# Score products of 512 columns issued as two matmuls of 256 with the same weights

## The chip, the cores and the metric

The kernel runs on one core of a Trainium2 chip, as one launch. A time is the device time of one execution in microseconds (us), and the median of several executions stands for a kernel. The core has five engines that run beside each other and wait for one another through semaphores: PE (TensorE, matmuls; its weight loads have a row of their own in the profile, PEld), DVE (VectorE), ACT (ScalarE), POOL (GpSimd) and SP (SyncE, which here issues most of the DMAs).

## The reference, cut to what matters

Four layers follow each other on a sequence of 2048 rows of 512 values, each with a residual: x = x + A(layernorm(x)), then B, then A, then B. A is a Fourier mixing: products with the DFT matrices of the hidden and of the sequence dimension, of which the real part is kept. B is attention with a compressed memory, in 32 heads of 16 values and 4 segments of 512 rows:

```python
for s in range(N):                                  # 4 segments, L = 512 rows each
    qs, ks, vs = q[:, :, s], k[:, :, s], v[:, :, s]
    logits = jnp.einsum("bhqd,bhkd->bhqk", qs, ks) * scale + mask   # causal mask
    p = _softmax(logits, axis=-1)
    a_dot = jnp.einsum("bhqk,bhkd->bhqd", p, vs)
    pq = phi(qs)                                    # phi(t) = t + 1 if t > 0 else exp(t)
    a_mem = (pq @ M) / (pq @ z + 1e-6)
    outs.append(g * a_mem + (1.0 - g) * a_dot)
    M, z = M + phi(ks).T @ vs, z + sum(phi(ks))
```

The change touches the logits, the products of queries and keys.

## The kernel before, in words

Everything is float32 to the outside. Most matmuls are made of three fp32r products of split values, high and low part (`matmul3`, line 107). The Fourier layers (lines 190 to 452) and the projections of attention are such products with 512 moving columns.

Attention (`place_attention`, line 454) works in units of four heads of one segment: 4 segments times 8 units, 32 units in each of the two attention layers, 64 in all. Queries and keys are split into three bf16 parts, written to DRAM and read back as stacks, `stkq` and `stkk` (`stack`, line 561), in which the parts stand one over another in 96 rows, so that one bf16 matmul with 96 rows gives a score with nearly float32 precision. A unit reads its stack twice:

- `natural_max` (line 581) computes scores with a row of queries on each partition, for query tiles i = 0 to 3 of 128 rows each. The weights are the query tile, the moving operand is the keys up to it: 128, 256, 384 or 512 columns. Two short products share a PSUM bank of 512 columns: 128 with 384, and 256 with 256 of two heads (the tile `nat`). DVE then adds the mask and takes the maximum of each row (line 603).
- `max_rows` (line 632) transposes these maxima and writes them, split in three bf16 rows, under the queries of the stack, where they are rows 97 to 99 (`KROWS` is 96, `K` 99).
- `softmax_values` (line 647) computes the scores again, with keys on the partitions and the maximum already taken off (tile `sT`). Weights are the key tile kt, moving columns are the queries from it on: 512, 384, 256 or 128. Again 384 shares a bank with 128, and 256 with 256 of the next head. ACT clips the diagonal blocks (Relu, line 668) and takes the exponent (line 669), POOL zeroes what the mask hides (line 672), and PE multiplies with the values (`pv`, line 682).

So each unit has four products of 512 columns in either form (i = 3, and kt = 0), 8 in all, and 512 in the kernel.

The order of the work is written out by slots: `place` (line 177) puts a step of a generator into a numbered slot, and at the end (lines 1056 to 1059) the slots run in order, within a slot by a rank. PE's instructions keep this program order (`in_order`, line 83). The other engines' order is the scheduler's, which goes by program order and by priorities: `tc.high_priority(offset=URGENT)` moves an instruction forward by a number of instructions (URGENT is 150, line 41). Besides the lines above, the prediction speaks of `prep` (line 458), which loads rows of the layer's input as `xt`, normalises them to `xn` (line 159) and transposes them for the next segment; of the output product (`po`, line 860, with the split values `oh`); and of SP's queue, which issues the loads of `xt`, the stacks and the parts in one order. In the prediction "fp32r" names the products of split values, "bf16" the scores.

Of the kernel before, what the change touches and what calls it, by code (L numbers as in the profile page):

```python
# [18 lines left out]
P = 128  # L19
# [16 lines left out]
KROWS = NSLOT * DH  # L36
# [25 lines left out]
def spectral_infini_kernel(  # L62
# [13 lines left out]
    V, A, G, T = nc.vector, nc.scalar, nc.gpsimd, nc.tensor  # L76
# [6 lines left out]
    def in_order(engine, name):  # L83
        op = getattr(engine, name)

        def call(*args, **kwargs):
            return tc.keep_in_program_order(op(*args, **kwargs))  # L87

        return call

    T = SimpleNamespace(matmul=in_order(T, "matmul"), transpose=in_order(T, "transpose"))
# [15 lines left out]
    def matmul3(ps, lhsT, rhs, first, last):  # L107
        T.matmul(ps, lhsT(0), rhs(0), start=first, stop=False)
        T.matmul(ps, lhsT(0), rhs(1), start=False, stop=False)
        T.matmul(ps, lhsT(1), rhs(0), start=False, stop=last)  # L110

    def rows(ap, i):
        return ap[i * P : (i + 1) * P, :]

    def bank(name, shape=(P, 512), dtype=F32):
        return psum.tile(list(shape), dtype, name=name, tag="bank", bufs=8)

    def pair(name, tag, bufs, dtype=F32R):
        return sb.tile([P, 2, 512], dtype, name=name, tag=tag, bufs=bufs)
# [334 lines left out]
    def place_attention(x_in, x_out, t0, w_at, out_at):  # L454
# [126 lines left out]
        def natural_max(s, g, u):  # L581
            qs, ks = stacks[s, g, u, "q"], stacks[s, g, u, "k"]
            mx = sb.tile([P, HU, LT], F32, name="mx", bufs=2)

            def scores(*cols):
                ps = bank("nat")
                views, off = [], 0
                for h, i in cols:
                    n = (i + 1) * P
                    T.matmul(  # L590
                        ps[:, off : off + n],
                        qs[:KROWS, h, i * P : (i + 1) * P],
                        ks[:KROWS, h, :n],
                        start=True,
                        stop=True,
                    )
                    views.append((ps[:, off : off + n], mx[:, h, i : i + 1]))
                    off += n
                for src, dst in views:
                    n = src.shape[1]  # L600
                    junk = sb.tile([P, 512], BF16, name="junk", bufs=1)
                    with tc.high_priority(offset=URGENT):
                        V.tensor_tensor_reduce(  # L603
                            junk[:, :n], src, mask[:, 512 - n :], 1.0, 3e38,
                            ALU.add, ALU.min, dst,
                        )

            for h in range(HU):
                scores((h, 3))
                yield  # L610
                scores((h, 0), (h, 2))
                yield
                if h % 2:
                    scores((h - 1, 1), (h, 1))
                    yield
            parts = max_parts[((s * NG + g) * (HG // HU) + u) % 2]
            rem = sb.tile([P, HU, LT], F32, name="mrem", bufs=2)
            with tc.high_priority(offset=2 * URGENT):
                V.scalar_tensor_tensor(
                    parts[:, 0], mx, -2.0, mx, op0=ALU.mult, op1=ALU.add  # L620
                )
                for dst in rem, parts[:, 1]:
                    V.scalar_tensor_tensor(
                        dst, mx, -1.0, parts[:, 0], op0=ALU.mult, op1=ALU.subtract
                    )
                V.scalar_tensor_tensor(
                    parts[:, 2], rem, 1.0, parts[:, 1], op0=ALU.mult, op1=ALU.subtract
                )
            maxima[s, g, u] = parts
            yield  # L630
# [16 lines left out]
        def softmax_values(s, g, u):  # L647
            qs, ks = stacks.pop((s, g, u, "q")), stacks.pop((s, g, u, "k"))
            K = KROWS + MROWS
            h0 = g * HG + u * HU  # L650

            def scores(dst, *cols):
                ps = bank("sT")
                off, diag = 0, []
                for h, kt in cols:
                    n = 512 - kt * P
                    T.matmul(
                        ps[:, off : off + n],
                        ks[:K, h, kt * P : (kt + 1) * P],
                        qs[:K, h, kt * P :],  # L660
                        start=True,
                        stop=True,
                    )
                    diag.append(off // P)
                    off += n
                blocks = ps.rearrange("p (b c) -> p b c", c=P)
                blocks = blocks[:, diag[0] : diag[-1] + 1 : max(1, diag[-1] - diag[0])]
                A.activation(blocks, blocks, AF.Relu)  # L668
                A.activation(dst, ps, AF.Exp, scale=-SCALE)  # L669

            def causal(blocks):
                G.affine_select(  # L672
                    blocks,
                    blocks,
                    pattern=[[0, n] for n in blocks.shape[1:-1]] + [[1, P]],
                    compare_op=ALU.is_ge,
                    fill=0.0,
                    base=0,
                    channel_multiplier=-1,
                )  # L680

            def pv(pv_bank, kt, pt, off):
                n = 512 - kt * P
                for h in range(HU):
                    T.matmul(
                        pv_bank[32 * h : 32 * h + VW, kt * P :],
                        vt[s][kt][:, h0 + h, :],
                        pt[h // 2][:, h % 2, off : off + n],
                        start=kt == 0,
                        stop=kt == 2,  # L690
                        skip_group_check=True,
                    )

            p0, p1 = [], []
            events = {}

            def ev(t, f):
                events.setdefault(t, []).append(f)

            for h in range(HU):  # L700

                def first(h=h):
                    if h % 2 == 0:
                        p0.append(pair("pT", "wd", 8, F32))
                    scores(p0[h // 2][:, h % 2], (h, 0))
                    if h % 2:
                        causal(p0[h // 2][:, :, :P])

                ev(6 + h, first)
            for h in range(HU):  # L710

                def second(h=h):
                    if h % 2 == 0:
                        p1.append(pair("pT", "wd", 8, F32))
                    scores(p1[h // 2][:, h % 2], (h, 1), (h, 3))
                    if h % 2:
                        for c in 0, 3 * P:
                            causal(p1[h // 2][:, :, c : c + P])

                ev(2 + h, second)  # L720
            p2 = []
            for h in range(0, HU, 2):

                def third(h=h):
                    if h == 0:
                        p2.append(sb.tile([P, HU, 256], F32, name="pT2", tag="craw", bufs=2))
                    scores(p2[0][:, h : h + 2].rearrange("p h s -> p (h s)"), (h, 2), (h + 1, 2))
                    if h == 2:
                        causal(p2[0][:, :, :P])

                ev(h // 2, third)

            def last():
                pb = pv_banks[0]
                pv(pb, 0, p0, 0)
                pv(pb, 1, p1, 0)
                pv(pb, 3, p1, 384)
                pv(pb, 2, (p2[0][:, :2], p2[0][:, 2:]), 0)
                ot = sb.tile([P, 512], F32, name="ot", tag="ut", bufs=8)
                A.activation(ot, pb, AF.Copy)  # L740
                outs[s, g, u] = ot

            ev(12, last)
            for t in range(13):
                for f in events.get(t, ()):
                    f()
                yield
# [196 lines left out]
        for k in range(4 * DT):  # L944
            n, d = "qkvo"[k // DT], k % DT
# [156 lines left out]
```

## Time and profile before

| | |
|---|---|
| median of 3 timed runs | 1908.67 us (1908.55 to 1909.09) |
| span of the profiled execution | 1911.1 us |
| mean granted clock of TensorE in it | 0.985 |
| instructions, PE / PEld / DVE / ACT / POOL | 10336 / 10336 / 4073 / 2292 / 831 |
| busy, PE / PEld / DVE / ACT / POOL | 95% / 68% / 69% / 56% / 27% |
| DMA | 296.49 MB, mean 155 GB/s |

The profile is of one execution, from its first to its last instruction; it is the only time that stands for this execution, and it is 2.4 us over the median of the timed runs. A row of a group names line, engine, operation, output and inputs, the shapes and the count, then the busy time in us, the mean duration of one in ns, and the idle time of the engine just before these instructions with what ended it. A row of a timeline gives start and duration in us. A matmul has its line in a helper (L87), so tiles tell the groups apart. Ends of matmuls are modelled and successive ones overlap, so a sum of durations is not a time on the engine.

### The profile page before, as it was taken

Reading aid. Unit: us, or ns where it says so; the run is one execution under the profiler, and the core shown is the slowest. Engines: PE = TensorE matmul, PEld = TensorE weight load, DVE = VectorE, ACT = ScalarE, POOL = GpSimd, SP = SyncE. Lnnn points to the kernel's source line nnn. Section 1 sums busy time; section 2 is a strip of 40 time slices with the busy share of each in tenths; the row PEclk is TensorE's granted clock in tenths of the full one; section 3 lists DMA queues with packets and bytes.
Section 4 is the critical chain, followed back from the end, with each engine's and each line's share of the span. In section 5 each row is a group of like instructions: output and inputs, shape, how many; then the busy total and the mean of one; then the engine's idle time right before and its main releaser. Section 6 shows DMA issues by size and latency. Waiting matters only on the chain. (4 is left out here: it accounts for less than half of the span.)

```text
span 1911.1 us, 31877 instructions
## 1 busy us (share of the span) xinstructions
PE 1809.7 (95%) x10336; PEld 1301.0 (68%) x10336; DVE 1311.1 (69%) x4073; ACT 1062.9 (56%) x2292; POOL 512.5 (27%) x831
## 2 busy tenths in 40 slices
PE   7899999999899999999889999999988999999998
PEld 6678888888556656665458888787865655666654
DVE  8654545462787787777866687777558778777773
ACT  3221213331578777767664465453337877777775
POOL 4200000002345344446431000000124443434432
PEclk9999999999899999999999999999999999999998
DMA  6665555353544333434445787563444434444231
GB/s 224 233 208 199 189 191 198 115 173 121 178 125 148 118 120 115 149 119 134 134 154 181 222 251 225 164 204 127 159 150 139 144 108 134 126 133 142 91 117 45
DMA packets 165655, 296.49 MB, mean 155 GB/s; under 512 B 17776, under 2 KB 66928, under 8 KB 165488
## 3 DMA queue, kind: packets, MB, share of 16 engines
q1 hardware_dynamic: 162224, 293.68, 47.5%
q8 instruction: 81, 1.33, 0.3%
q10 hardware_dynamic: 3264, 0.79, 0.2%
q14 instruction: 86, 0.70, 0.1%
HBM read 192.95 MB, written 100.66 MB: 154 GB/s over the span
## 5 line engine op out<-in xcount | busy, mean ns | idle before, releaser
L603 DVE CUSTOM_DVE_ANT_0 junk<-nat,mask 128x512 bf16<-128x512 f32 (+3 forms) x1024 | 496.6, 485 | 203.2 <-PE nat L87 183.9
L669 ACT ACTIVATE pT<-sT 128x512 f32<-128x512 f32 x640 | 370.3, 598 | 15.0 <-ACT sT L668 2.2
L87 PE MATMUL u<-chi,xa 128*128 128x512 f32 x1024 | 321.1, 395 | 10.9 <-DVE xa L97 7.3
L672 POOL TENSOR_SCALAR_AFFINE_SELECT pT<-pT 128x256 f32<-128x256 f32 (+1 forms) x448 | 197.4, 455 | 431.5 <-ACT pT L669 366.8
L87 PE MATMUL sT<-stkq,stkk 99*128 99x256 bf16 (+3 forms) x1024 | 250.7, 307 | 17.5 <-DVE mx L603 8.8
L87 PE MATMUL nat<-stkk,stkq 96*128 96x512 bf16 (+3 forms) x1024 | 246.5, 302 | 20.8 <-DVE mx L603 12.4
L668 ACT ACTIVATE sT<-sT 128x256 f32<-128x256 f32 (+1 forms) x640 | 208.6, 334 | 63.9 <-PE sT L87 56.7
L87 PEld LDWEIGHTS u<-chi,xa 128*128 128x128 f32 x1024 | 195.4, 191 | 52.8 <-issue 7.2
L87 PE MATMUL u<-clo,xa 128*128 128x512 f32 x512 | 202.6, 396 | 9.6 <-DVE clo L101 9.6
L142 POOL TENSOR_TENSOR r<-ve,half_neg 128x2 f32<-128x2 f32 (+1 forms) x33 | 24.0, 728 | 696.5 <-DVE ve L140 692.9
L87 PE MATMUL y<-wdt,us 128*128 128x512 f32 x768 | 182.5, 391 | 1.2 <-DVE wdt L101 1.2
L87 PEld LDWEIGHTS <-stkk 99*128 99x128 bf16 x1024 | 82.6, 99 | 146.3 <-issue 127.9
L87 PEld LDWEIGHTS y<-wdt,us 128*128 128x128 f32 x768 | 143.4, 188 | 31.6 <-DVE wdt L101 2.0
L87 PE MATMUL pv_bank<-pT,vt 128*17 128x128 f32 (+3 forms) x2048 | 158.7, 440 | 1.7 <-POOL pT L672 1.6
L87 PEld LDWEIGHTS <-stkq 96*128 96x128 bf16 x1024 | 94.9, 99 | 75.9 <-issue 37.3
L87 PE MATMUL po<-wo,oh 128*128 128x512 f32 x384 | 125.7, 443 | 7.6 <-DVE oh L101 5.4
L87 PE MATMUL pvv<-wv,xT 128*128 128x512 f32 x384 | 127.0, 443 | 3.9 <-DVE mx L603 3.9
L87 PE MATMUL pqk<-xT,wq 128*128 128x512 f32 x384 | 129.9, 447 | 0.0
L87 PE MATMUL pqk<-xT,wk 128*128 128x512 f32 x384 | 127.8, 442 | 0.0
L87 PEld LDWEIGHTS u<-clo,xa 128*128 128x128 f32 x512 | 97.7, 191 | 32.5 <-DVE clo L101 12.2
L87 PEld LDWEIGHTS pv_bank<-pT,vt 128*17 128x17 f32 x2048 | 57.6, 98 | 90.7 <-issue 77.0
L99 ACT ACTIVATE clo<-cring 128x512 fp32r<-128x512 f32 x112 | 70.6, 631 | 69.1 <-DVE chi L101 37.9
(138 smaller groups left out, 3032.0 us busy)
## 6 DMA issues: line engine op xcount, KB each, us to landing
sum<-sring SPq DMA_DIRECT2D x32, 1024.0 KB
cring<-sum SPq DMA_DIRECT2D x128, 256.0 KB
stkq<-scrq SPq DMA_DIRECT2D x64, 384.0 KB
stkk<-scrk SPq DMA_DIRECT2D x64, 384.0 KB
cring<-in_ct SPq DMA_DIRECT2D x96, 256.0 KB
sring<-in_ct SPq DMA_DIRECT2D x32, 512.0 KB
xt<-mid SPq DMA_DIRECT2D x64, 256.0 KB
craw<-in_ct SPq DMA_DIRECT2D x30, 512.0 KB
```

The costliest lines, as they stand in the source:

```text
L87: return tc.keep_in_program_order(op(*args, **kwargs))
L99: A.activation(hi, src, AF.Copy, scale=scale)
L142: G.tensor_tensor(out=r, in0=ve, in1=half_neg[:, :n], op=ALU.pow)
L603: V.tensor_tensor_reduce(junk[:, :n], src, mask[:, 512 - n :], 1.0, 3e38, ALU.add, ALU.min, dst,)
L668: A.activation(blocks, blocks, AF.Relu)
L669: A.activation(dst, ps, AF.Exp, scale=-SCALE)
L672: G.affine_select(blocks, blocks, pattern=[[0, n] for n in blocks.shape[1:-1]] + [[1, P]], compare_op=ALU.is_ge, fill=0.0, base=0, channel ...
```

## The change

A product of 512 moving columns is issued as two of 256, with the same weights, into the two halves of the same PSUM bank. Products of 128, 256 and 384 columns stay as they are, and so does everything that reads the results.

```diff
+    def halves(n):
+        return ((0, n // 2), (n // 2, n // 2)) if n == 512 else ((0, n),)
...
                     n = (i + 1) * P
-                    T.matmul(
-                        ps[:, off : off + n],
-                        qs[:KROWS, h, i * P : (i + 1) * P],
-                        ks[:KROWS, h, :n],
-                        start=True,
-                        stop=True,
-                    )
+                    for c, w in halves(n):
+                        T.matmul(
+                            ps[:, off + c : off + c + w],
+                            qs[:KROWS, h, i * P : (i + 1) * P],
+                            ks[:KROWS, h, c : c + w],
+                            start=True,
+                            stop=True,
+                        )
...
                     n = 512 - kt * P
-                    T.matmul(
-                        ps[:, off : off + n],
-                        ks[:K, h, kt * P : (kt + 1) * P],
-                        qs[:K, h, kt * P :],
-                        start=True,
-                        stop=True,
-                    )
+                    for c, w in halves(n):
+                        T.matmul(
+                            ps[:, off + c : off + c + w],
+                            ks[:K, h, kt * P : (kt + 1) * P],
+                            qs[:K, h, kt * P + c : kt * P + c + w],
+                            start=True,
+                            stop=True,
+                        )
```

In the built program each bf16 matmul has a weight load instruction of its own, so either half loads the weights again.

## The prediction, made before the changed kernel ran

> **What bounds the kernel now.** I read the first two parts of the page, then the busy time by stretch, then the groups by shape, then the timeline of the score products. The page:
>
> ```profile
> span 1911.1 us, 31877 instructions
> PE 1809.7 (95%) x10336; PEld 1301.0 (68%) x10336; DVE 1311.1 (69%) x4073; ACT 1062.9 (56%) x2292; POOL 512.5 (27%) x831
> ```
>
> PE is the busiest engine by far, and it has one weight load (PEld) for each matmul. The score products stand in the two attention stages; their busy time by stretch (columns: stretch, its us, busy us of PE, PEld, DVE, ACT and POOL with instruction counts, granted clock, DMA share, GB/s):
>
> ```profile
> 500.00:1005.00 505.00, 466.76 (x3230) 293.24 (x3230) 387.64 (x1552) 377.49 (x885) 230.81 (x388) 0.97 0.42 132
> 1415.00:1911.00 496.00, 458.82 (x3233) 287.08 (x3231) 365.85 (x1509) 364.88 (x863) 203.24 (x364) 0.98 0.38 121
> ```
>
> Of these 1001 us PE is idle for 38.2 + 37.2 = 75.4 us. So PE is the bound in both, nine tenths of the time: what lengthens PE's stream there lengthens the kernel, nearly one for one. The groups of the score products, by shape (busy us, mean ns of one):
>
> ```profile
> L87 PE MATMUL sT<-stkq,stkk 99*128 99x512 bf16 x256 | 100.3, 393 | 2.4 <-ACT pT L669 1.4 <-DVE mx L603 1.0
> L87 PE MATMUL nat<-stkk,stkq 96*128 96x512 bf16 x256 | 98.1, 383 | 10.0 <-DVE mx L603 6.2 <-DMA stkk<-scrk 2.7 <-DVE onat L806 0.4
> L87 PE MATMUL sT<-stkq,stkk 99*128 99x256 bf16 x256 | 51.7, 284 | 12.0 <-DVE mx L603 4.9 <-ACT oh L99 2.6 <-DMA stkq<-mt 2.5
> L87 PE MATMUL nat<-stkk,stkq 96*128 96x256 bf16 x256 | 49.6, 275 | 0.0
> ```
>
> These means are not what a product costs the stream. 284 + 284 against 393 looks like a loss of 175 ns for each split, but matmuls are pipelined, and a mean of one contains its way through the array, which lies under the next one. The cost is the time from one start to the next. Happily the kernel already issues pairs of 256 columns, each with its own weight load, beside singles of 512, in the same places of the stream, so that the trace of before holds the very thing that the change makes.
>
> **The change, part by part.** It removes 256 + 256 = 512 matmuls of 512 columns and adds 1024 of 256, with 512 more weight loads. The price of one split comes from start to start. Timeline of PE (start, us, instruction, count); for each kind the first and the last row of those that I averaged, with the row that follows each:
>
> ```profile
> 497.66 0.38 PE L87 MATMUL sT<-stkq,stkk 99*128 99x256 bf16 x2
> 497.88 0.38 PE L87 MATMUL nat<-stkk,stkq 96*128 96x512 bf16 x1
> ...
> 500.19 0.39 PE L87 MATMUL nat<-stkk,stkq 96*128 96x256 bf16 x2
> 500.41 0.38 PE L87 MATMUL sT<-stkq,stkk 99*128 99x384 bf16 x2
> ...
> 524.38 0.39 PE L87 MATMUL sT<-stkq,stkk 99*128 99x512 bf16 x1
> 524.61 0.38 PE L87 MATMUL nat<-stkk,stkq 96*128 96x128 bf16 x2
> ...
> 540.67 0.38 PE L87 MATMUL nat<-stkk,stkq 96*128 96x512 bf16 x1
> 540.89 0.38 PE L87 MATMUL sT<-stkq,stkk 99*128 99x512 bf16 x1
> ...
> 1865.63 0.39 PE L87 MATMUL sT<-stkq,stkk 99*128 99x512 bf16 x1
> 1865.86 0.38 PE L87 MATMUL nat<-stkk,stkq 96*128 96x256 bf16 x2
> 1866.08 0.38 PE L87 MATMUL sT<-stkq,stkk 99*128 99x512 bf16 x1
> ...
> 1868.39 0.39 PE L87 MATMUL sT<-stkq,stkk 99*128 99x256 bf16 x2
> 1868.62 0.38 PE L87 MATMUL nat<-stkk,stkq 96*128 96x512 bf16 x1
> 1868.84 0.38 PE L87 MATMUL sT<-stkq,stkk 99*128 99x256 bf16 x2
> ```
>
> Transposed scores (sT) behind a 512-column fp32r product, at the full clock and without a wait: a single takes 524.61 - 524.38 = 0.23 us at the first and 0.23 at the last, over 154 of them a mean of 227.7 ns (median 227); a pair 0.22 and 0.23, over 69 a mean of 229.5 (median 230). Natural scores (nat) ahead of another bf16 product or a small one: a single 0.22 and 0.22, over 24 a mean of 220.0 (median 219); a pair 0.22 and 0.22, over 59 a mean of 221.5 (median 222). So a split costs 1.5 to 1.8 ns by the means and 3 by the medians. I take 2 ns: 512 x 2 = **+1.0 us**. The bounds are 0 (the last rows of both kinds are alike to the 0.01 us that the timeline shows) and 3 ns, which is 0 and +1.5 us; 2 ns is nearest to the means, and a sum is made of means.
>
> The weight loads lie beside the matmuls:
>
> ```profile
> L87 PEld LDWEIGHTS <-stkq 96*128 96x128 bf16 x1024 | 94.9, 99 | 75.9 <-issue 37.3 <-DVE onat L806 0.7
> L87 PEld LDWEIGHTS <-stkk 99*128 99x128 bf16 x1024 | 82.6, 99 | 146.3 <-issue 127.9 <-DMA stkq<-mt 9.4 <-DVE mx L603 0.9
> ```
>
> A load takes 99 ns, and a half of 256 columns holds the array for some 110 (half of the 0.22 above): the load of the second half fits under the first half. I cost the 512 loads at nothing; the matmul before each hides it, and if that cover were gone they would cost 512 x 99 ns = 50.7 us. [...]
>
> The change adds no wait: in the built program the first half takes over the wait of the single, the second waits for nothing, and only the second half signals. So ACT's Relu of the diagonal block, which reads only columns of the first half in the kt = 0 products, cannot start on the first half; I count no gain there. Readers of a whole product see it 113 + 275 against 383 ns after its start (113 is half of a 0.22 to 0.23 pair, rounded up), so about 5 ns later; if each of the 512 stood on the path, 2.6 us, but DVE and ACT have slack in most places, and I take 0.
>
> What moves on the other engines: PE's order stays as it is but for the halves. About a dozen instructions of DVE, four of ACT, three of POOL and four transfers on SP's queue change places with neighbours, because the scheduler counts the new instructions. The place that matters is where attention prepares its last segment (line 159, xn), in both layers; the first layer's (an [idle before <-releaser] behind a row is that engine's wait):
>
> ```profile
> 676.47 0.32 SPq L574 DMA_DIRECT2D stkq<-scrq  x1
> ...
> 677.50 0.68 DVE L603 CUSTOM_DVE_ANT_0 junk<-nat,mask 128x512 bf16<-128x512 f32 x1
> ...
> 678.11 1.28 DVE L159 TENSOR_SCALAR xn<-xt,mv,rr 128x512 f32<-128x512 f32 x2
> ...
> 678.24 0.38 PE L87 MATMUL sT<-stkq,stkk 99*128 99x256 bf16 x2 [0.67 <-DVE mx L603]
> ...
> 680.25 0.38 PE L87 MATMUL nat<-stkk,stkq 96*128 96x512 bf16 x1 [1.64 <-DVE mx L603]
> ...
> 681.99 1.65 PE L87 MATMUL po<-wo,oh 128*128 128x512 f32 x3 [1.36 <-DVE oh L101]
> ```
>
> One xn (0.64 us) now runs ahead of the 512-column maximum, so PE's wait of 0.67 us grows by 0.64. The next wait, for a maximum behind both xn, ends where it did, and 1.64 shrinks to 1.0: net 0. On SP one load of xt, which waits for that first xn (by these rows it would end near 677.50 + 0.64 = 678.1), goes ahead of the stack loads that left at 676.47, so those leave some 2 us later. The first score product that reads them, and the same two events of a usual unit behind it:
>
> ```profile
> 690.16 0.38 PE L87 MATMUL nat<-stkk,stkq 96*128 96x512 bf16 x1
> ...
> 1652.62 0.33 SPq L574 DMA_DIRECT2D stkq<-scrq  x1
> ...
> 1660.08 0.38 PE L87 MATMUL nat<-stkk,stkq 96*128 96x512 bf16 x1
> ```
>
> 13.7 us of lead become about 11.7, still more than the 7.5 us of the usual unit, where PE does not wait. I take 0 for all moves; their bounds are rivals A and D below.
>
> The sum: 1.0 us on the span of 1911.1 us gives 1912.1. The timed runs have a median of 1908.67, 2.4 us under the profiled span, and I carry the difference over: 1908.67 + 1.0 = **1909.7 us**, +0.05%. About 0.2% (3.8 us) is what a measurement of this kernel can tell from no change.
>
> **The rivals.** *A, slower: a stall that costs the clock.* Right behind the stall above, and behind its like in the second layer, PE runs at half the clock; busy time by stretch:
>
> ```profile
> 678.00:681.10 3.10, 0.75 (x3) 0.19 (x2) 3.06 (x9) 2.87 (x7) 2.44 (x3) 1.00 0.79 177
> 681.10:687.90 6.80, 5.92 (x22) 3.45 (x26) 4.29 (x12) 1.80 (x4) 1.22 (x2) 0.50 0.77 273
> ...
> 1609.50:1612.90 3.40, 3.40 (x17) 2.40 (x19) 2.07 (x6) 0.37 (x2) 0.00 (x0) 0.50 1.06 384
> ```
>
> 6.8 and 3.4 us at 0.50 cost up to 3.4 and 1.7 us. If a moved instruction of DVE makes a stall longer by one xn (0.64) where nothing gives it back, and as much half clock again follows, that is 4.0 us in the first layer and 2.3 in the second: 1908.67 + 1.0 + 6.4 = 1916.1. It decides once PE's idle time in such a place, 3.7 us now (0.67 + 1.64 + 1.36), grows instead of shifting. For it: the moves stand just there. Against: the releasers of the last two waits keep their places.
>
> *B, slower: instructions do not reach PE fast enough.* The densest long stretch and a usual one:
>
> ```profile
> 807.28:827.28 20.00, 20.00 (x165) 13.33 (x164) 15.26 (x63) 13.09 (x31) 7.16 (x14) 1.00 0.49 161
> 1700.00:1800.00 100.00, 98.58 (x723) 64.10 (x722) 75.61 (x317) 77.54 (x183) 46.42 (x83) 1.00 0.42 136
> ```
>
> 329 matmuls and loads in 20 us are one per 60.8 ns; the usual is 1445 in 100 us, 69.2 ns. If 60.8 were a ceiling, the 512 x 2 new instructions would cost up to 62 us where all is that dense; on the average of 69.2 there is room (7% more gives 64.5), so perhaps a fifth of it, 12 us: 1921. Nothing shows PE starved in that stretch (20.00 busy of 20.00), which speaks against. [...]
>
> [...]
>
> *D, faster: the same shuffle goes the other way.* An earlier xn shortens one of PE's waits enough that the half-clock stretch does not come, in both layers: 1908.67 + 1.0 - 3.4 - 1.7 = 1904.6, just past 0.2%. For it: waits there hang on DVE. Against: 1.36 us behind oh remain in any case.
>
> **How the numbers follow.** Forecast (0 to 3 ns for each split, the moves give nothing that lasts) 0.70; A 0.14; B 0.04; C 0.03; D 0.09. Range 1905 to 1917: the upper end takes in A with both layers (1916.1), the lower end all of D's way but its last step; B, C and D, 0.16 in all, are left out. Faster by over 0.2%: D, 0.09; slower: A, B and C, 0.21; within: 0.70.
>
> **What would show it.** In the profile after, PE and PEld should count 10848 each, no score product of 512 columns should be left, and 768 of 256 should stand in either group, the pairs taking 0.22 to 0.23 us from start to next start and the busy time of DVE, ACT and POOL as before. [...] I am wrong about the term itself if the pair of one product, which loads the same weights twice, differs from the pair of two products that I measured.

## The result, and the profile after

| | before | after |
|---|---|---|
| median of 20 runs each, taken in turn on the same chip | 1907.62 us | 1912.21 us |
| lowest and highest run | 1902.87, 1910.96 | 1906.47, 1917.94 |
| span of the profiled execution | 1911.1 us | 1908.5 us |

The ratio is 1.0025, with a 95% interval of 1.0016 to 1.0034: slower by 4.6 us by the medians. The forecast was +1.0 us. The time lies in the range that was given, but just over the 0.2% that the forecast called no change, and the interval reaches down to 0.16%, so the side of that line is not sure. That the change costs something is.

The two profiled executions say the opposite of the medians: after is 2.6 us shorter. The execution profiled for after took 1910.26 us, below the median of its 20 runs, and the one of before lay above its own median. Runs of one kernel spread over 8 to 11 us here, so one profile against one profile decides nothing of this size. What profiles can decide is what the work costs where it stands. The page of after, its busy time by engine:

```profile
span 1908.5 us, 33070 instructions
PE 1806.2 (95%) x10848; PEld 1330.2 (70%) x10848; DVE 1309.1 (69%) x4073; ACT 1062.8 (56%) x2292; POOL 511.8 (27%) x831
```

512 matmuls and 512 loads more; DVE, ACT and POOL have the same instructions and the same busy time to 2 us. The groups of 256 columns (busy us, mean ns of one, idle time before them):

```profile
L87 PE MATMUL sT<-stkq,stkk 99*128 99x256 bf16 x768 | 151.4, 280 | 16.3 <-DMA stkq<-mt 7.5 <-DVE mx L607 6.9 <-ACT pT L674 1.3
L87 PE MATMUL nat<-stkk,stkq 96*128 96x256 bf16 x768 | 148.2, 274 | 7.5 <-DVE mx L607 4.5 <-DMA stkk<-scrk 1.8 <-DVE onat L811 0.4
```

768 in either form, as forecast, and no group of 512 columns is left. The two attention stages (columns as in the prediction):

```profile
500.00:1005.00 505.00, 465.14 (x3496) 307.70 (x3495) 389.51 (x1558) 379.82 (x889) 230.34 (x388) 0.99 0.42 133
1415.00:1908.50 493.50, 458.50 (x3474) 303.18 (x3473) 364.39 (x1506) 363.77 (x862) 202.88 (x363) 0.97 0.39 121
```

PEld is busier by 14 and 16 us, PE by nothing (465.14 us against 466.76, 458.50 against 458.82): the loads lie under the matmuls. PE's timeline in the second attention layer, with the former singles as pairs:

```profile
1687.98 0.38 PE L87 MATMUL nat<-stkk,stkq 96*128 96x256 bf16 x2
1688.12 0.94 PE L87 MATMUL pqk<-xT,wq 128*128 128x512 f32 x3
1688.90 0.40 PE L87 MATMUL sT<-stkq,stkk 99*128 99x256 bf16 x2
1689.13 0.38 PE L87 MATMUL nat<-stkk,stkq 96*128 96x128 bf16 x2
```

The pair of one product takes 1689.13 - 1688.90 = 0.23 us to the next start, as the pairs of two products did in before. A natural pair with the three fp32r products behind it takes 0.92 us.

### The profile page after: what moved, and what is told of

It is laid out like the page before. It is cut to its first block, busy times and chain, and to the rows that moved or that the text cites. A ratio compares the mean times of both kernels' runs of the same rounds, so it can differ in the third digit from the quotient of the medians.

```text
span 1908.5 us, 33070 instructions
## 1 busy us (share of the span) xinstructions
PE 1806.2 (95%) x10848; PEld 1330.2 (70%) x10848; DVE 1309.1 (69%) x4073; ACT 1062.8 (56%) x2292; POOL 511.8 (27%) x831
## 5 line engine op out<-in xcount | busy, mean ns | idle before, releaser
L87 PE MATMUL sT<-stkq,stkk 99*128 99x256 bf16 (+2 forms) x1280 | 250.5, 278 | 17.4 <-DVE mx L607 7.8
L87 PE MATMUL nat<-stkk,stkq 96*128 96x256 bf16 (+2 forms) x1280 | 247.0, 274 | 17.2 <-DVE mx L607 12.1
L87 PEld LDWEIGHTS <-stkk 99*128 99x128 bf16 x1280 | 93.5, 99 | 149.0 <-issue 130.5
L87 PEld LDWEIGHTS <-stkq 96*128 96x128 bf16 x1280 | 113.6, 99 | 60.9 <-issue 33.0
L87 PE MATMUL pvv<-wv,xT 128*128 128x512 f32 x384 | 120.7, 426 | 3.8 <-DVE mx L607 3.8
L87 PE MATMUL pqk<-xT,wk 128*128 128x512 f32 x384 | 122.6, 428 | 0.0
L87 PE MATMUL pqk<-xT,wq 128*128 128x512 f32 x384 | 121.8, 426 | 0.0
L99 ACT ACTIVATE clo<-cring 128x512 fp32r<-128x512 f32 x112 | 70.6, 631 | 69.1 <-DVE chi L101 37.1
```

The costliest lines, as they stand in the source:

```text
L99: A.activation(hi, src, AF.Copy, scale=scale)
```

## The experiments

Theories. **T1**: the split itself costs PE's stream 1 to 5 us. **T2**: the split costs about nothing, and the changed order on the other engines carries the loss, through stalls and the half clock behind them (rival A's mechanism, in some place). Beside them rival B (instructions arrive too slowly) and C (the second load shows) were carried on.

In each comparison the kernel before ran on the same chip in the same rounds; a1 to a4 ran on one chip, b1 to b4 on a second, c1 to c4 on a third. The edit that most kernels share pins an engine's order. The numbers are an engine's instructions in program order, and each gets a scheduling edge, without a semaphore, to its neighbour:

```diff
+    pinned = {
+        "SP": [[210, 211, 247, 214, 213, 212], ...],
+        "DVE": [[847, 1042, 853, 1043, ...], [1281, 1282, 1283, 1410, 1411, 1284], [2436, 2631, ...]],
+        "Activation": [[2293, 2294, 2295, 2297, ...]],
+    }
+    for engine, runs in pinned.items():
...
+            for a, b in zip(run, run[1:]):
+                tc.add_manual_dep(traced[b], traced[a].name, ...)
```

The order of before and that of after differ in four groups of moves: *prep* (DVE's first and third list, and SP's four, both attention layers), *spectral* (DVE's second list: one `xn` of the second Fourier layer's `normalise` ahead of one maximum, and with it two splits on POOL), and the *tail* (ACT's list, near the end). In the traces DVE, ACT, POOL and SP follow the order that each experiment names, instruction for instruction.

### Two by two: the split and the order

**a1**, the kernel before with no edit, shows what the comparison gives for nothing.

> The kernel before, unchanged, as a fourth corner of a table of two by two (products whole or split; the other engines' order of before or of after). Every theory: a ratio of 1.000 to the kernel before, within 0.1%; what it differs by is the noise of the other three.

**a2**, whole products in the order of after:

```diff
+        "DVE": [[847, 1042, 1043, 853, ...], [1281, 1282, 1410, 1283, 1411, 1284], [2436, 2631, 2632, ...]],
```

> Products whole as before, but DVE, ACT, POOL and SP in the order that the scheduler gives them in the changed kernel (pinned). Theory M, that the moved instructions cost what the split does not (the measured 4.6 us less 1.0): a ratio of 1.0019, about +3.6 us. Rival S, that the split itself costs all of the 4.6 us, in ways that one profile does not show: 1.000.

**a3**, the split in the order of before (the first diff above, on the kernel after).

> Products split as in the changed kernel, but DVE, ACT, POOL and SP in the order of the kernel before (pinned). Theory M: only the stream cost of the split, 512 x 2 ns = 1.0 us, a ratio of 1.0005. Rival S: 1.0024, about +4.6 us, 9 ns for each split.

**a4**, the kernel after again, no edit.

> The changed kernel once more. Both theories: 1.0024 as measured; a ratio under 1.001 would mean that the first comparison was of two draws of noise (theory N).

**c4**, a3 once more, on another chip.

> The split with the old order once more, to narrow the cost of the split alone: theory M 1.0005 (+1.0 us), within 1.000 and 1.001; a ratio of 1.0015 or more would put the loss back on the split.

Measured, ratio to the kernel before with its interval:

| | order of before | order of after |
|---|---|---|
| whole | a1 0.9998 (0.9984 to 1.0012) | a2 1.0015 (0.9999 to 1.0030) |
| split | a3 1.0001 (0.9985 to 1.0017), c4 0.9998 (0.9986 to 1.0010) | a4 1.0032 (1.0017 to 1.0046), the result 1.0025 (1.0016 to 1.0034) |

The split alone costs nothing that can be measured, twice; with the new order the loss is there, twice. T1 in its larger sizes falls (the upper ends of a3 and c4 are 3.2 and 1.9 us, which leaves room for the forecast's 1.0), and the order is where the loss lies. The new order on whole products gives 1.0015, which is consistent with anything from nothing to the whole loss.

The split's own cost is best read in a dense stretch. The second attention layer has one from a transposition of maxima (`mT`) to another nine units on, at the full clock, with 72 split products; start of its first and last row in before, in after, and in b4 (below, the same products in quarters):

```profile
1691.61 0.22 PE L87 MATMUL mT<-ident_b,mparts 128*80 128x128 bf16 x1
...
1826.21 0.22 PE L87 MATMUL mT<-ident_b,mparts 128*80 128x128 bf16 x1 [0.17 <-DVE mx L603]
```

```profile
1689.35 0.22 PE L87 MATMUL mT<-ident_b,mparts 128*80 128x128 bf16 x1
...
1823.82 0.22 PE L87 MATMUL mT<-ident_b,mparts 128*80 128x128 bf16 x1 [0.17 <-DVE mx L607]
```

```profile
1689.94 0.22 PE L87 MATMUL mT<-ident_b,mparts 128*80 128x128 bf16 x1
...
1825.46 0.22 PE L87 MATMUL mT<-ident_b,mparts 128*80 128x128 bf16 x1 [0.17 <-DVE mx L607]
```

134.60 us before, 134.47 after, 135.52 in quarters. Nine units of halves cost nothing that this shows; 2 ns each would be 0.14 us, which is about the size by which the two differ in the other direction.

### Which of the moves

**b1**, the split with only the prep moves as in after (the lists for prep are dropped, so the scheduler places these as in after; the others stay pinned):

```diff
-        "SP": [...],
-        "DVE": [[847, ...], [1281, 1282, 1283, 1410, 1411, 1284], [2436, ...]],
+        "DVE": [[1281, 1282, 1283, 1410, 1411, 1284]],
```

> Products split; DVE and SP in the new order where attention prepares its last segment (xn, the statistics and the loads of xt, in both layers), everything else in the old order. If these moves carry the loss of the new order: a ratio of 1.002 to 1.003 to the kernel before; if not: 1.000. By the waits at 678 us I had priced this group at nothing, so I lean to 1.000.

Measured 1.0002 (0.9990 to 1.0015). The place that the prediction named costs nothing.

**b2**, the split with only the spectral move new:

```diff
-        "DVE": [[847, ...], [1281, 1282, 1283, 1410, 1411, 1284], [2436, ...]],
+        "DVE": [[847, ...], [2436, ...]],
```

> Products split; only the one xn of DVE and the two splits of POOL that moved at the start of the second Fourier layer (near 950 us) in the new order. If this group carries the loss: 1.002 to 1.003; if not: 1.000. The profiles of the new order have a longer wait of PE for POOL near 970 us, which speaks for it.

Measured 1.0013 (1.0002 to 1.0025): +2.3 us by the medians, the only one of the three that stands clear of 1.

**b3**, the split with only the tail new:

```diff
-        "Activation": [[2293, 2294, 2295, 2297, ...]],
```

> Products split; only the four instructions of ACT near the end (from 1865 us) in the new order. If this group carries the loss: 1.002 to 1.003; if not: 1.000. The two profiles with the old order from the second chip have no half clock behind 1876 us, the two with the new order have, which speaks for it.

Measured 1.0003 (0.9993 to 1.0013). The sign that spoke for it does not hold: a1 and a3, with the old order, do run at half clock at the very end (from 1902.8 and 1899.3 us), and b1, with the old tail, also from 1875.7 us.

**c1**, the counterpart of b2: the kernel after, with the spectral move alone put back:

```diff
+    pinned = {"DVE": [[1281, 1282, 1283, 1410, 1411, 1284]]}
```

> Products split, all moves of the new order but the one near 950 us (an xn of DVE, two splits of POOL), which is back in its old place. If that move is the main carrier, as its 1.0013 alone said: 1.0005 to 1.001; if the loss is spread or comes of all together: 1.0015 or more.

Measured 1.0002 (0.9988 to 1.0015). One instruction of DVE put back behind one maximum, and no loss is seen; a4 and the result, which differ from c1 only in this move and the two splits on POOL that go with it, have 1.0032 and 1.0025. Those two ran on other chips than c1, and the kernel after was not run on c1's chip, so that the loss would have shown there is taken over from them.

**c2**, the kernel before with the spectral move alone made:

```diff
+    pinned = {"DVE": [[1281, 1282, 1410, 1283, 1411, 1284]]}
```

> Products whole, only the move near 950 us in the new order: the suspected carrier without the split. If it carries the loss by itself: 1.001 to 1.0015, as with the split; if it needs the split: 1.000.

Measured 0.9991 (0.9976 to 1.0006). On whole products the same move costs nothing that can be measured. So by c1 it is needed for the loss, and by c2 it does not make it alone. The two whole kernels with this move do not agree well (c2 0.9991, a2 1.0015 with the other moves too), on two chips; their intervals overlap a little.

Some expectations put this place near 950 us; that was a misreading, the traces have it at 880 to 890 us. Here is what it does. The chain is DVE's `xn`, POOL's subtraction on it (line 208 before, 211 after), ACT's high part `xa` (L99), and POOL's low part `xa` (L101), which reads `xn` last and so frees one of its two buffers. Timelines of POOL, DVE, ACT and PE in before, in that order (start, us; in brackets the wait):

```profile
883.87 2.58 POOL L101 TENSOR_TENSOR xa<-xn,xa 128x512 fp32r<-128x512 f32 x2 [0.42 <-ACT xa L99]
886.81 0.96 POOL L208 TENSOR_TENSOR xn<-xn 128x256 f32<-128x256 f32 x1 [0.36 <-DVE xn L159]
```

```profile
883.93 0.56 DVE L603 CUSTOM_DVE_ANT_0 junk<-nat,mask 128x384 bf16<-128x384 f32 x1
...
885.20 1.99 DVE L159 TENSOR_SCALAR xn<-xt,row_mv,row_r 128x512 f32<-128x512 f32 x2 [0.70 <-POOL xa L101]
```

```profile
863.58 0.22 PE L87 MATMUL mT<-ident_b,mparts 128*80 128x128 bf16 x1
...
891.16 0.38 PE L87 MATMUL nat<-stkk,stkq 96*128 96x128 bf16 x2 [2.25 <-ACT pT L669]
891.37 0.60 PE L87 MATMUL on<-ident,ot 128*128 128x128 f32 x4
...
966.57 0.25 PE L87 MATMUL mT<-ident_b,mparts 128*80 128x128 bf16 x1 [1.26 <-DVE mparts L626]
```

And in after, POOL, DVE, ACT and PE:

```profile
880.85 1.28 POOL L101 TENSOR_TENSOR xa<-xn,xa 128x512 fp32r<-128x512 f32 x1 [0.42 <-ACT xa L99]
882.80 0.73 POOL L211 TENSOR_TENSOR xn<-xn 128x256 f32<-128x256 f32 x1 [0.66 <-DVE xn L162]
883.49 1.27 POOL L101 TENSOR_TENSOR xa<-xn,xa 128x512 fp32r<-128x512 f32 x1
```

```profile
882.17 0.55 DVE L162 TENSOR_SCALAR xn<-xt,row_mv,row_r 128x512 f32<-128x512 f32 x1 [1.30 <-POOL xa L101]
882.63 0.55 DVE L607 CUSTOM_DVE_ANT_0 junk<-nat,mask 128x384 bf16<-128x384 f32 x1
...
884.79 0.83 DVE L162 TENSOR_SCALAR xn<-xt,row_mv,row_r 128x512 f32<-128x512 f32 x1 [1.60 <-POOL xa L101]
```

```profile
887.46 0.63 ACT L99 ACTIVATE xa<-xn 128x512 fp32r<-128x512 f32 x1 [3.27 <-POOL xn L211]
```

```profile
860.57 0.22 PE L87 MATMUL mT<-ident_b,mparts 128*80 128x128 bf16 x1
...
886.49 0.38 PE L87 MATMUL nat<-stkk,stkq 96*128 96x128 bf16 x2 [0.58 <-DVE mx L607]
889.54 0.74 PE L87 MATMUL on<-ident,ot 128*128 128x128 f32 x4 [2.67 <-ACT pT L674]
...
964.14 0.25 PE L87 MATMUL mT<-ident_b,mparts 128*80 128x128 bf16 x1 [1.25 <-DVE mparts L630]
```

Take the `mT` as the common zero. The first `xn`, although it was moved ahead, starts at 882.17 - 860.57 = 21.6 us, just as in before (885.20 - 863.58 = 21.6): it waits for POOL either way, only now with the maximum of 384 columns behind it. POOL, which in before freed both buffers in one go, now puts the subtraction between its two splits, and the second `xn` waits 1.60 us for the other buffer. ACT's queue stands 3.27 us before the `xa` that hangs on it, and the exponents `pT` stand behind that in the queue. PE waits 0.58 + 2.67 = 3.25 us in place of 2.25, and reaches `on` at 28.97 us in place of 27.79: **1.2 us later**. By the `mT` 103 us on, 0.6 of it is left in these two profiles (103.57 against 102.99), but the same way takes 102.05 us in a3, 104.51 in c1 and 105.98 in c4, all with the old place, so what is left further on cannot be read from them. The wait itself is in every profile: the five kernels with the move (after, a2, a4, b2, c2) have 0.58 to 0.60 and 2.67 to 2.68 us, the others one wait of 2.05 to 2.25. c1, with the old order, has the rows of before again:

```profile
885.69 1.99 DVE L162 TENSOR_SCALAR xn<-xt,row_mv,row_r 128x512 f32<-128x512 f32 x2 [0.69 <-POOL xa L101]
```

```profile
891.65 0.38 PE L87 MATMUL nat<-stkk,stkq 96*128 96x128 bf16 x2 [2.22 <-ACT pT L674]
```

c2, with whole products and without a loss, has the rows of after:

```profile
886.10 0.38 PE L87 MATMUL nat<-stkk,stkq 96*128 96x128 bf16 x2 [0.60 <-DVE mx L603]
889.16 1.04 PE L87 MATMUL on<-ident,ot 128*128 128x128 f32 x4 [2.68 <-ACT pT L669]
```

So the stall comes with the move, whether products are split or whole, and by itself it does not show in c2's time, of which the upper end is +1.1 us.

A microsecond is not 4.6. How the rest divides can be asked only over many runs. Each run lists its time and its mean granted clock. Where the clock is either full or half, as in the stretches of before and after (1.00 or 0.50), the time at half clock is 2 x (1 - clock) x time, and half of it is what the half clock cost if PE was the bound. Means over runs, with standard errors:

| kernels | runs | time, us | at half clock, us | time less half of that, us |
|---|---|---|---|---|
| whole, order of before (the kernel before beside the experiments, a1) | 111 | 1906.4 | 51.3 ± 0.8 | 1880.7 ± 0.3 |
| split, order of before (a3, c4) | 24 | 1906.0 | 48.8 ± 1.7 | 1881.6 ± 0.5 |
| whole, order of after (a2) | 12 | 1907.7 | 53.4 ± 1.8 | 1881.0 ± 0.4 |
| whole, spectral move alone (c2) | 12 | 1905.8 | 47.0 ± 1.3 | 1882.3 ± 0.9 |
| split, prep alone new (b1) | 12 | 1907.0 | 52.8 ± 2.4 | 1880.6 ± 0.7 |
| split, tail alone new (b3) | 11 | 1907.1 | 52.0 ± 2.3 | 1881.1 ± 0.9 |
| split, all but the spectral move new (c1) | 12 | 1907.4 | 51.2 ± 1.5 | 1881.8 ± 0.5 |
| split, spectral move alone (b2) | 12 | 1908.7 | 55.7 ± 1.7 | 1880.8 ± 0.7 |
| split, order of after (after, a4) | 32 | 1911.6 | 56.0 ± 1.2 | 1883.6 ± 0.4 |

The last row stands 5.2 us over the first: (56.0 - 51.3)/2 = 2.4 us of it is half clock and 2.9 us is not. The split without the new order adds 0.9 ± 0.6 us to the last column, the forecast's 1.0. Of the rows of this table, the two that have both the split and the spectral move (b2; after and a4) have the most half clock. That part would fit T2 with rival A's mechanism, in another place. The larger part would not: it is not half clock, and neither b2 (1880.8) nor a2 (1881.0) has it in the last column. And this is a sorting of means and no experiment: how the two together bring more half clock, and where in the run, was not settled, and b2, with both, shows only 2.3 us of the loss. The profiles do not place it either, since the time at half clock is not the same from one execution to the next: the mean granted clock went from 0.982 to 0.993 over the runs of the kernel before beside the experiments, and from 0.983 to 0.989 over those of after and a4. Right behind the stall, PE runs at half clock for 3.4 us in before (from 892.7 us) as in after (from 890.0 us), and for 6.8 us in b2.

### Larger doses of instructions

**b4**, products of 512 columns in quarters of 128, order of before:

```diff
-        return ((0, n // 2), (n // 2, n // 2)) if n == 512 else ((0, n),)
+        return tuple((c, P) for c in range(0, n, P)) if n == 512 else ((0, n),)
```

> Products of 512 columns issued as four of 128 (1536 matmuls and loads more than before, three times the change), the other engines pinned to the order of before. Theory M, that PE takes the pieces nearly free: a step of 128 takes 55 to 60 ns in the trace, so four take 220 to 240 against 220 to 227 ns, 0 to 6.7 us in all, a ratio of 1.000 to 1.0035. Rival B, a ceiling of one instruction per 60.8 ns: the usual stretch would hold 1757 instead of 1445 instructions per 100 us, 107 us of issue, about +68 us, 1.035. Rival C, loads not hidden: 1536 x 99 ns = +152 us, 1.08.

Measured 1.0024 (1.0014 to 1.0034), +3.7 us by the medians for 1536 more matmuls and loads than before.

**c3**, every score product in pieces of 128, order of before but for two exchanges on POOL:

```diff
+        return tuple((c, P) for c in range(0, n, P))
```

> Every score product issued in pieces of 128 columns (3072 matmuls and loads more than before, six times the change), the other engines in the order of before but for two exchanges on POOL. Theory M: four of 128 cost some 9 ns more than one of 512 by the run with quarters, so 3072 more pieces cost about 3072 x 3 = 9 us: 1.005. Rival B, one instruction per 60.8 ns at most: 2067 instead of 1445 in 100 us is 126 us of issue, +250 us: 1.13.

Measured 1.0100 (1.0077 to 1.0124), +18.5 us for 3072 more. Its page:

```profile
span 1926.0 us, 38258 instructions
PE 1832.9 (95%) x13408; PEld 1405.9 (73%) x13408; DVE 1316.6 (68%) x4073; ACT 1065.7 (55%) x2292; POOL 512.7 (27%) x831
```

And the stretch that the prediction called usual, in c3:

```profile
1700.00:1800.00 100.00, 97.99 (x1005) 73.65 (x1002) 74.60 (x310) 75.59 (x176) 40.88 (x74) 1.00 0.39 123
```

2007 matmuls and loads in 100 us are one per 49.8 ns, and rival B had 3.5% for the one and 13% for the other kernel: there is no ceiling near 60.8 ns per instruction. By the same sorting of runs as above, the time less half of the half clock is 1885.0 and 1897.8 us, 4.3 and 17.1 over the first row of the table: these costs are not the clock, and are put down to PE's stream (c3 has four runs only). They do not go by the count either: the first 1536 matmuls cost 4.3 us, the next 1536 12.8. A place where pieces of 128 columns do cost something stands in PE's timeline of b4:

```profile
1706.19 0.39 PE L87 MATMUL nat<-stkk,stkq 96*128 96x128 bf16 x4
1706.38 0.94 PE L87 MATMUL po<-wo,oh 128*128 128x512 f32 x3
1707.16 0.60 PE L87 MATMUL xnT<-ident,xn 128*128 128x128 f32 x4
...
1709.90 0.38 PE L87 MATMUL nat<-stkk,stkq 96*128 96x256 bf16 x2
1710.04 0.94 PE L87 MATMUL po<-wo,oh 128*128 128x512 f32 x3
1710.82 0.60 PE L87 MATMUL xnT<-ident,xn 128*128 128x128 f32 x4
...
1711.25 0.39 PE L87 MATMUL sT<-stkq,stkk 99*128 99x128 bf16 x4
1711.48 0.39 PE L87 MATMUL nat<-stkk,stkq 96*128 96x128 bf16 x4
```

Both natural groups are 512 columns with the same three fp32r products behind them. To `xnT` the four pieces of 128 take 0.97 us, the two of 256 take 0.92: 50 ns more. Four transposed pieces, with bf16 products behind, take 0.23 us as ever. So the extra time comes between a piece of 128 columns and the fp32r product behind it, whose weight loads are twice as long as those of a score (99 ns); the group of these loads in b4:

```profile
L87 PEld LDWEIGHTS po<-wo,oh 128*128 128x128 f32 x384 | 67.1, 194 | 19.9 <-DVE oh L101 6.9 <-DVE mx L607 2.2 <-issue 1.2
```

The account is not closed: b4's trace has some 200 such natural groups ahead of fp32r products, at the full clock and without a wait, and at 50 ns each they come to 10 us, where b4 lost 4.3. PE is idle for 95.1 us in b4's profile, against 99.1 and 97.1 in a3 and c4, so shorter waits gave some of it back.

No kernel of the study beats the kernel before by more than its interval.

## Why the prediction was right or wrong

**The split's price** (2 ns each, +1.0 us): right. Two runs of the split in the old order give 1.0001 and 0.9998, and the means without half clock 0.9 ± 0.6 us. The pairs that before already had were the right model, and the pair of one product, which loads the same weights twice, behaves like the pair of two.

**Weight loads hidden**: right. PEld is 29 us busier (1330.2 us against 1301.0), and the pairs of split products in after, which load the same weights twice, still take 0.23 us from start to next start, so rival C (the second load shows; 512 loads of 99 ns would be 50.7 us, an estimate from the trace of before) falls. How the second load comes to lie under the first half, no run here shows.

**No wait added by the split**: nothing speaks against it; the split in the old order is as fast as before.

**The moves at prep**: nearly right in their net of 0, and b1 finds no cost. PE at that place, first attention layer; the first row is of before, the others of after:

```profile
672.49 0.22 PE L87 MATMUL mT<-ident_b,mparts 128*80 128x128 bf16 x1
```

```profile
670.13 0.22 PE L87 MATMUL mT<-ident_b,mparts 128*80 128x128 bf16 x1
...
674.59 0.38 PE L87 MATMUL nat<-stkk,stkq 96*128 96x128 bf16 x2 [0.50 <-DVE mx L607]
...
676.54 0.38 PE L87 MATMUL sT<-stkq,stkk 99*128 99x256 bf16 x2 [0.88 <-DVE mx L607]
...
678.11 0.39 PE L87 MATMUL nat<-stkk,stkq 96*128 96x256 bf16 x2 [1.19 <-DVE mx L607]
...
679.85 1.65 PE L87 MATMUL po<-wo,oh 128*128 128x512 f32 x3 [1.35 <-DVE oh L101]
```

The wait that was to grow by 0.64 grew by 0.21, and one of 0.50 us came in ahead of it, for an earlier maximum, which the prediction did not have; the next shrank by 0.45 in place of 0.64, and the last stayed. From `mT` to `po` PE takes 679.85 - 670.13 = 9.72 us, against 681.99 - 672.49 = 9.50 before: 0.2 us more, not 0. The stack loads on SP's queue went as forecast: in after they leave at 676.32 us, 2.2 us later behind this `mT` than before, and the score product that reads them starts at 687.73 without a wait, a lead of 11.4 us where 11.7 was forecast. The half clock behind the waits is as long as it was, 6.8 us:

```profile
678.30:685.10 6.80, 5.45 (x20) 3.28 (x22) 4.25 (x11) 1.86 (x5) 1.50 (x2) 0.50 0.93 289
```

In the second layer there are 6.8 us (from 1603.4 us) in place of 3.4 in this execution, which the prediction would have read as rival A. Read alone, that sign misleads: b1, which has exactly these moves, gives 1.0002, and c4, in the order of before, has 6.8 us there too.

**"The place that matters is where attention prepares its last segment (line 159, xn), in both layers"**, and with it **"I take 0 for all moves"**: this is the step that failed. The move on which the loss hangs is the one that was counted among "about a dozen instructions of DVE" and "three of POOL" and not worked out: the `xn` of the second Fourier layer with POOL's two splits. The trace of before had its rows at 883 to 891 us, with DVE waiting 0.70 us for POOL's `xa` and PE 2.25 us behind ACT. Worked out like prep, they say that an `xn` that waits for a buffer gains nothing by being moved ahead, and delays what stands behind it. That would have priced the place at about +1 us. c1 against a4 and the result, on different chips, puts 0.23 to 0.30% on it when the other moves and the split are there too; the stall that the profiles show is not that large, and it is there in c2 without a loss. That the time fell inside the range is luck: the upper end was set by rival A at prep, and that is not what happened.

**Rival A** had the wrong place, and a price of 6.4 us over the split where 3.6 was found. Its mechanism, a stall and the half clock behind it, is at most a part: by the table 2.4 us of the loss are half clock, and that the stall brings them is not shown. **B and C** fell with b4 and c3, **D** did not come. Four pieces of 128 columns, each with its own load, take 0.23 us in b4 (1711.48 - 1711.25), 57 ns for a piece, and c3 has one matmul or load per 49.8 ns where the densest long stretch of before had one per 60.8; b4's 1536 more loads cost 3.7 us in all, where C expected 152. **What stays open**: why the spectral move costs nothing on whole products (c2), though the stall is the same, and less alone (b2) than with the other moves; what makes up the 2.9 us that are not half clock, beyond the split's 0.9; at which places the additional half clock falls; and whether the loss is the same on the chips of b1 to b4 and c1 to c4, where the kernel after was not run.

## What to carry to other kernels

Where the same pair already stands in the trace, its start-to-start time prices a split far better than means of durations do: here about 2 ns a split against 175 by the means, and the runs give 0.9 ± 0.6 us for the 512. When an edit changes the number of instructions, list every instruction that the scheduler then moves on the other engines and price each at its own place: look first for one that waits for a buffer, since moving it ahead only holds up what stands behind it in the queue (here `xn` started 21.6 us behind `mT` as before, and PE reached `on` 1.2 us later). And compare such small effects over many runs with the orders pinned, since single profiles differed here by more than the effect, and in the wrong direction.

## What the runs showed of the hardware

- The half clock is not the same from one run to the next of one kernel: the mean granted clock of the runs of after went from 0.984 to 0.989, and each 0.001 is 3.8 us more or less at half clock, of which about half is lost, by the estimate of the table of means. This makes up much of the spread of 8 to 11 us: over the runs of one kernel, time and clock are correlated at -0.7 in the 20 runs of after and at -0.8 in the 35 of before beside the first four experiments.
- In b4 a group of 512 columns in pieces of 128 with fp32r products behind it takes 50 ns more than one in pieces of 256 (0.97 against 0.92 us). That fits the longer load of an fp32r product, 194 ns against 99, which the short piece may not cover; that the load is the cause was argued from these rows, and not tried by itself.
- PE was fed 13408 matmuls and as many loads within 1926.0 us in c3, 71.8 ns for each instruction on the average and 49.8 ns in the stretch from 1700 to 1800 us, where it was busy for 97.99 of 100 us.
